# Two layers of sliding-window attention and MLP: W2's transfers, three evictions, masks and sums in other places of a hand-written order

## The chip, the cores and the metric

The kernel runs on one core of one Trainium2 chip. The metric is the time of one execution on the device, in microseconds (us). A core has five engines with a queue of instructions each: TensorE (PE: matrix products and transposes), VectorE (DVE), ScalarE (ACT), GpSimd (POOL) and SyncE (SP), which here only issues DMA transfers. Each engine takes its instructions strictly in order, and waits on semaphores for what the others produce.

## What is computed

The input `x` is 2048 rows of 512 numbers in bf16. Two layers, each of attention and an MLP, are applied one after the other, with the same weights:

```python
def _A_ref(x, wqkv, wo):                      # H = 32 heads of Dh = 16, window W = 256
    q, k, v = ...                             # x @ wqkv, split by head
    scores = jnp.einsum("bhqd,bhkd->bhqk", q, k) * (Dh ** -0.5)
    mask = (idx[:, None] - idx[None, :] >= 0) & (idx[:, None] - idx[None, :] < W)
    scores = jnp.where(mask[None, None], scores, -1e9)
    p = _softmax(scores, axis=-1)
    o = jnp.einsum("bhqk,bhkd->bhqd", p, v)
    return ... @ wo

def _B_ref(x, w1, b1, w2, b2):                # 512 -> 1792 -> 512
    h = _gelu(jnp.einsum("bsd,df->bsf", x, w1) + b1)
    return jnp.einsum("bsf,fd->bsd", h, w2) + b2

x = A_x
x = x + _A_ref(_layernorm(x), A_wqkv, A_wo)
x = x + _B_ref(_layernorm(x), B_w1, B_b1, B_w2, B_b2)
x = x + _A_ref(_layernorm(x), A_wqkv, A_wo)
x = x + _B_ref(_layernorm(x), B_w1, B_b1, B_w2, B_b2)
```

## The kernel before

**Blocks and jobs.** Each attention layer is cut into 8 blocks of 256 rows, so blocks 0 to 7 are layer one and 8 to 15 layer two. A block has two row tiles of 128 rows; row tiles are numbered 0 to 31 over both layers. The MLP goes by jobs of two or four row tiles. The normalizations are numbered 0 to 31 ahead of attention and 32 to 63 ahead of the MLP, so 32, 33 and 48 belong to MLP rows and 8, 9 and 25 to attention rows.

**One block of attention**, with the names that the prediction uses (`b` the block, `tau` the row tile, `k` the normalization):

- `bs`, `ba`, `ve`/`vp`, `pw`: statistics, mean and variance, and the reciprocal root of a row tile. `xn{k}` (L606, DVE) is the normalized tile, `tx{k}` (L611, SP) the DMA that transposes it into `xnTA` (ahead of attention) or `xnTB` (ahead of the MLP).
- `q{b}_{i}`, `k{b}_{i}`, `v{tau}`: the projections (`pe_group`, L632, PE). Each goes into one bank of PSUM and is evicted: `qe{b}_{i}` to `QT` and `ve{tau}` to `Va` by a copy, either VectorE's (L573, in the profile CAST) or ScalarE's (L575, ACTIVATE); `ke{b}_{i}` to `KT` (L666, DVE) with a multiplication by a mask of parities. `vs{tau}_{h}` (L681, SP) are two DMAs that copy `Va` shifted by 64 rows to `Vs`.
- `sc{b}_{g}`: the scores of visit `g` (L733, PE) into four banks, two for each of the two exponentials `ex{b}_{g}_{0,1}` (L740, ACT, 128x1024 to `E`). `mk{b}_{g}_{n}` (L761) multiplies parts of `E` by the mask, on VectorE or GpSimd. A block has 10 visits (5 in the first block of a layer).
- `pv{b}_{cp}`: the product with V for one half of the heads (L783, PE), after half of the visits; then `od` (L792, DVE transpose out of PSUM), `rc` (L796, reciprocal), `nm` (L800, division, DVE or POOL) and `ot` (L806, DVE transpose to `OT`).
- `op{tau}`: the product with Wo (L632), and `rs{tau}` (L832, DVE), which adds it to `X`.

**One job of the MLP.** Each of 14 columns of W1 gives a bank; the gelu is `ge{J}_{fc}` (L863, ACT), or `gb` (L855, DVE, the bias) followed by `ga` (L858, ACT). `y{tau}.{fc}` are the 14 matmuls with W2 (L632); `xb{tau}` (L871, POOL) prepares X plus the bias, and `ya{tau}` (L875, DVE) adds it to the product.

**Loads.** All weights are loaded once. W2 comes in four parts `ldz0` to `ldz3` (L563, SP): rows fc 0–3, 4–7, 8–10 and 11–13. SP's queue also holds every `tx` and `vs`. It issues in order, and a DMA takes one of eight semaphores in turn, so it first waits for the DMA eight places ahead of it.

**What sets the order.** The code registers 3080 nodes, each with an engine, its reads and its writes. `_ORDER` (from L167) is a list, written out, of all 3080 numbers; `_Plan.run` takes the nodes in this order, `_Sched.op` (L62) puts each behind the others of its engine and adds the waits that its data need. So `_ORDER` sets the order in every engine's queue, though a change in it that does not swap two nodes of one engine changes nothing. `_ALT` (from L323) lists the nodes that take their other engine: a copy of an eviction then goes from VectorE to ScalarE, a mask from VectorE to GpSimd, a variance from GpSimd to VectorE. `_BANKS` is the list of PSUM banks in the order in which they are taken.

**The places that are touched**, by queue. In block 1, `sc1_7` follows `sc1_6` in TensorE's queue and takes the banks of `ex1_5` and of `od1_0`. On ScalarE before it stand ex1_4_0, ex1_4_1, ex1_5_1, ex1_5_0, qe3_0, ex1_6_1, ex1_6_0, ex1_7_0. Later in that stage TensorE does k4_0 (needs `xn8`, `tx8`), then job 0's `ge0_9` ends, `y1` (14 matmuls) and `pv1_1` follow. In block 10 VectorE does xn48, rs19 and mk10_4_0, then ke11_1; TensorE has sc10_5, which waits for rs19, and sc10_6, which waits for ke11_1.

Of the kernel before, what the change touches and what calls it, by code (L numbers as in the profile page):

```python
# [19 lines left out]
class _Sched:  # L20
# [300 lines left out]
]  # L321

_ALT = [  # L323
# [623 lines left out]
```

## Time and profile before

| | before |
|---|---|
| time, median of 3 runs | 456.76 us (456.69 to 457.06) |
| time of the profiled execution | 457.15 us |
| its span (first to last instruction in the trace) | 455.3 us |
| mean clock granted to TensorE | 0.996 |
| instructions | 16,821 |
| DMA packets | 47,972, 23.25 MB |
| slices of the 40 in which TensorE is busy under 80% | four: the 10th (5 tenths), 11th, 12th and 16th (7 tenths) |

The profile is one execution of the kernel on the chip. A line of a group of instructions names the engine, the line of the kernel, the operation, the tile written and read, the shape, the count, and behind a bar the time; in the timeline a line begins with its start in us and its duration, and ends, in square brackets, with the idle time of the engine ahead of it and the work that ended it. Where lines are grouped, `x4` is a count, and the duration is that of the whole group.

### The profile page before, as it was taken

How to read it: one execution, taken by the hardware profiler on the slowest of the kernel's cores; microseconds unless marked ns; L12 is line 12 of the kernel's file. 1: busy time of each engine (PE TensorE's matmuls, PEld its weight loads, DVE VectorE, ACT ScalarE, POOL GpSimd, SP SyncE). 2: the span in 40 equal slices, each digit the busy share in tenths (PEclk: the TensorE clock that was granted, in tenths of full speed). 3: DMA queues.
4: the chain of work that ended last, by engine and by line, in shares of the span. 5: the costliest groups of instructions: out<-in, count | busy, mean ns of one | idle time of the engine just before them, and what ended most of it. 6: DMA issues, size and time to landing. Idle time of an engine off the chain costs nothing.

```text
span 455.3 us, 16821 instructions
## 1 busy us (share of the span) xinstructions
PE 420.6 (92%) x7506; PEld 230.2 (51%) x7579; DVE 352.7 (77%) x655; ACT 385.0 (85%) x456; POOL 193.4 (42%) x217
## 2 busy tenths in 40 slices
PE   8998999985779997899999999999999999999997
PEld 4564646543344553445455454555554454444673
DVE  5999689886775778894799867977897598756862
ACT  2997968987889899789998998999888989899633
POOL 4164634237331247632472754274243443526130
PEclk9999999999899999999999999999999999999999
DMA  8695311201400211310012021010232003002110
GB/s 243 186 218 166 77 33 24 44 10 18 86 15 1 25 23 41 76 26 1 14 35 58 1 56 37 10 42 3 62 50 62 1 4 79 14 1 67 60 48 24
DMA packets 47972, 23.25 MB, mean 51 GB/s; under 512 B 33180, under 2 KB 47900, under 8 KB 47900
## 3 DMA queue, kind: packets, MB, share of 16 engines
q1 hardware_dynamic: 47900, 22.17, 21.0%
q8 instruction: 60, 0.98, 0.9%
q14 instruction: 12, 0.10, 0.1%
HBM read 8.00 MB, written 2.10 MB: 22 GB/s over the span
## 4 chain that ended last, share of the span: by engine, by line
PE 69%; DVE 15%; ACT 12%; issue 3%; DMA 2%; POOL 0%; SPq 0%
PE ps L632 52%; ACT E L740 11%; PE ps L733 8%; PE ps L783 7%; DVE KT L666 2%; DVE E L761 2%; DVE OD L792 2%; DVE xn L606 2%; PE ps L525 1%; DVE stat L584 1%; DMA xnTB<-xn 1%; DVE OT L806 1%; DVE X L832 1%; DMA xnTA<-xn 1%; DVE X L875 1%
## 5 line engine op out<-in xcount | busy, mean ns | idle before, releaser
L740 ACT ACTIVATE E<-ps 128x1024 bf16<-128x1024 f32 x300 | 283.1, 1041 | 42.4 <-PE ps L733 41.7
L761 POOL TENSOR_TENSOR E<-E,mask 128x512 bf16<-128x512 bf16 (+2 forms) x97 | 104.2, 1089 | 88.1 <-ACT E L740 88.0
L632 PE MATMUL ps<-xnTB,W_sb 128*128 128x512 bf16 (+1 forms) x542 | 110.2, 335 | 4.2 <-issue 1.6
L632 PE MATMUL ps<-W_sb,gT 128*128 128x512 bf16 x415 | 110.1, 380 | 3.3 <-issue 2.2
L761 DVE TENSOR_TENSOR E<-E,mask 128x512 bf16<-128x512 bf16 (+2 forms) x139 | 70.1, 529 | 10.3 <-ACT E L740 10.1
L632 PE MATMUL ps<-xnTA,Wqkv_sb 128*128 128x256 bf16 x512 | 74.6, 273 | 2.1 <-ACT E L740 0.7
L632 PEld LDWEIGHTS ps<-xnTB,W_sb 128*128 128x128 bf16 x560 | 50.6, 97 | 44.7 <-issue 4.1
L733 PE MATMUL ps<-QT,KT 32*128 32x128 bf16 (+3 forms) x1920 | 60.4, 232 | 10.9 <-ACT E L740 2.9
L632 PEld LDWEIGHTS ps<-W_sb,gT 128*128 128x128 bf16 x448 | 39.6, 98 | 43.2 <-issue 3.6
L733 PEld LDWEIGHTS ps<-QT,KT 32*128 32x128 bf16 x1920 | 28.6, 93 | 62.5 <-ACT E L740 36.9
L632 PEld LDWEIGHTS ps<-xnTA,Wqkv_sb 128*128 128x128 bf16 x512 | 46.9, 98 | 25.3 <-issue 3.9
L792 DVE STREAM_TRANSPOSE OD<-ps 128x1024 f32<-128x1024 f32 x32 | 39.8, 1244 | 21.5 <-PE ps L783 21.2
L863 ACT ACTIVATE gT<-ps,b1T 128x512 bf16<-128x512 f32 (+1 forms) x80 | 43.6, 609 | 10.3 <-PE ps L632 9.9
L871 POOL TENSOR_TENSOR Xb<-X,b2all 128x512 f32<-128x512 bf16 x32 | 38.5, 1209 | 24.8 <-DVE X L875 24.8
L783 PE MATMUL ps<-E,Va 64*17 64x128 bf16 (+3 forms) x1920 | 44.0, 230 | 4.1 <-ACT E L740 1.8
L666 DVE TENSOR_TENSOR KT<-ps,parmask 128x1024 bf16<-128x1024 f32 x32 | 38.8, 1212 | 11.1 <-PE ps L632 10.8
L783 PE MATMUL ps<-E,Vs 64*17 64x128 bf16 (+3 forms) x1920 | 44.6, 230 | 0.0
L783 PEld LDWEIGHTS ps<-E,Va 64*17 64x17 bf16 x1920 | 37.4, 84 | 13.9 <-issue 8.8
L584 DVE BATCH_NORM_STATS2 stat<-X 128x6 f32<-128x512 bf16 x64 | 42.7, 677 | 1.8 <-DMA X<-in_A_x_dram 1.7
L855 DVE TENSOR_SCALAR gT<-ps,b1T 128x512 bf16<-128x512 f32 (+1 forms) x60 | 36.5, 629 | 7.0 <-PE ps L632 6.4
L800 POOL TENSOR_TENSOR Nb<-OD,Rc 128x512 bf16<-128x512 f32 x19 | 20.2, 1061 | 49.9 <-DVE Rc L796 39.6
L632 PE MATMUL ps<-Wo_sb,OT 128*128 128x512 bf16 x120 | 37.2, 388 | 3.4 <-DVE OT L806 2.5
(50 smaller groups left out, 363.0 us busy)
## 6 DMA issues: line engine op xcount, KB each, us to landing
Vs<-Va SPq DMA_DIRECT2D x64, 68.0 KB, 2.1
W_sb<-in_B_w_dram SPq DMA_DIRECT2D x4, 512.0 KB, 5.5
out_dram<-X SPq DMA_DIRECT2D x16, 128.0 KB, 1.9
X<-in_A_x_dram SPq DMA_DIRECT2D x3, 512.0 KB, 7.3
Wqkv_sb<-in_A_wqkv_dram SPq DMA_DIRECT2D x4, 256.0 KB, 5.3
W_sb<-in_B_w_dram SPq DMA_DIRECT2D x1, 768.0 KB, 6.5
W_sb<-in_B_w_dram SPq DMA_DIRECT2D x2, 384.0 KB, 4.8
Wqkv_sb<-in_A_wqkv_dram SPq DMA_DIRECT2D x1, 512.0 KB, 7.1
```

The lines of the kernel that those rows point to most:

```text
L584: add("dve", lambda e, B, t=t, k6=k6: e.bn_stats(stat6[:, k6, :], X[:, t, :]), reads=["X%d" % t], writes=["st%d" % k6], key="bs%d" % (k + j))
L632: r = e.matmul(ps[:, B[g][0], cols], lhsT, rhs, start=st, stop=sp)
L666: add("dve", lambda e, B, g=g, i=i: e.tensor_tensor(out=KT[:, kb, 2 * i : 2 * i + 2].rearrange("p c m a q -> p a (c m) q"), in0=ps[:, B[g] ...
L733: x = e.matmul(ps[:, bk[r], o : o + n], KT[rows, kb, c, m].rearrange("p a q -> p (a q)"), QT[rows, c, q : q + n], start=True, stop=True)
L740: add("act", lambda e, B, g_=g_, gi=gi: e.activation(E[:, 2 * gi : 2 * gi + 2, e0 : e0 + 512], ps[:, B[g_][0] : B[g_][0] + 2, :], AF.Exp, ...
L761: fn = lambda e, B: e.tensor_tensor(out=Ew, in0=Ew, in1=Mw, op=ALU.mult)
L783: x = e.matmul(ps[32 * r : 32 * r + VW, B[g][par], c % 2 * 2 * P + lo : c % 2 * 2 * P + hi], V[rows, (2 * b + m // 2) % VR, c * HC + 2 * r ...
L792: add("dve", lambda e, B: e.transpose(OD[:, s].rearrange("p a c q -> p (a c q)"), ps[:, B[g][0] : B[g][0] + 2, :]), reads=["ps:" + g], wri ...
L800: return e.tensor_tensor(out=Nb[:, s, :].rearrange("p (k a d) -> p a k d", a=2, d=Dh), in0=sums[:, :, :, 0:Dh], in1=rc[:, :, :, None].to_b ...
L855: add("dve", lambda e, B, g=g, fc=fc: e.tensor_scalar(out=gT[:, fc, c0 : c0 + M], in0=ps[:, B[g][0], 0:M], scalar1=b1T[:, fc : fc + 1], sc ...
L863: add("act", lambda e, B, g=g, fc=fc: e.activation(gT[:, fc, c0 : c0 + M], ps[:, B[g][0], 0:M], AF.Gelu_apprx_tanh, bias=b1T[:, fc : fc + ...
L871: add("pool", lambda e, B, t=t, xs=xs: e.tensor_tensor(out=Xb[:, xs, :], in0=X[:, t, :], in1=b2all[:], op=ALU.add), reads=["X%d" % t, "b2a ...
```

## The change

No instruction is added or removed but for those that go to another engine; TensorE's queue and the PSUM banks are the same. By queue:

- **To another engine** (`_ALT`): `ve5` and `qe3_1`, copies of 128x512 out of PSUM, from VectorE to ScalarE; `mk10_3_0`, a mask of block 10, from GpSimd back to VectorE.
- **ScalarE**: `qe3_0` moves ahead of the exponentials ex1_5, `ve5` takes the place behind them, and `qe3_1` stands behind ex1_6. The order is then ex1_4_1, qe3_0, ex1_5_1, ex1_5_0, ve5, ex1_6_1, ex1_6_0, qe3_1, ex1_7_0.
- **VectorE, the first 45 us**: `i6` (a constant) ahead of te3, `ba7` and `ba6` some five places earlier, `ve1` four places later, bs33 ahead of bs32.
- **GpSimd, block 1**: `xb1` and `mk1_7_0` from ahead of mk1_6_0 to behind mk1_5_0. The order is then nm1_0, mk1_6_0, xb0, mk1_8_0, mk1_8_1, mk1_5_0, xb1, mk1_7_0, mk1_7_1.
- **SP, loads of W2**: before, ldz1, ldz2, ldz0, tx32, tx33, vs5_0, vs6_0, vs5_1, tx9, tx8, ldz3, vs4_1, vs7_1; after, tx32, tx33, ldz0, ldz1, vs5_0, vs6_0, vs5_1, tx9, tx8, ldz2, ldz3, vs4_1, vs7_1.
- **VectorE, block 10**: after, xn48, `mk10_3_0`, rs19, bs51, bs50, ba51, vp26, `mk10_4_0`, ba50, vp50, ke11_1; before, mk10_4_0 stood straight behind rs19.
- **VectorE, other blocks**: xn25 ahead of od9_1, `ot11_0` ahead of the masks mk12_2_0 and mk12_0_0 (straight behind od11_1), xn56 ahead of ya21.

The other moves in `_ORDER` swap nodes of different engines only. The diff, cut to the stretches named here (node numbers: ldz0 to ldz3 50 to 53, tx32 242, tx33 244, qe3_0 336, qe3_1 341, ve5 191, xb1 306, mk1_7_0 405, mk10_3_0 2066, mk10_4_0 2071, rs19 1854, ot11_0 2197, xn56 2503, xn25 2014):

```diff
--- before.py
+++ after.py
@@ -165,42 +165,42 @@
...
-    384, 234, 378, 185, 228, 385, 332, 229, 333, 51, 383, 342, 187, 386, 52, 334, 235, 377, 343, 335, 50, 237, 344,
-    337, 394, 388, 345, 396, 382, 338, 188, 238, 236, 387, 189, 239, 190, 395, 346, 339, 240, 389, 336, 191, 398, 243,
-    641, 347, 400, 348, 349, 241, 340, 350, 390, 399, 242, 352, 359, 527, 244, 402, 391, 341, 392, 351, 353, 192, 403,
-    354, 306, 355, 360, 356, 361, 404, 407, 639, 357, 362, 409, 363, 193, 248, 405, 249, 262, 528, 250, 263, 408, 412,
...
+    234, 378, 185, 228, 385, 332, 229, 333, 383, 342, 187, 237, 386, 334, 377, 343, 335, 235, 344, 336, 337, 388, 394,
+    345, 382, 396, 338, 238, 236, 188, 387, 189, 239, 190, 346, 395, 339, 240, 389, 191, 243, 641, 398, 241, 347, 400,
+    390, 348, 242, 349, 340, 350, 399, 352, 527, 359, 244, 391, 351, 341, 392, 402, 353, 403, 354, 50, 355, 401, 360,
+    356, 361, 404, 407, 639, 51, 362, 290, 409, 363, 248, 192, 249, 262, 357, 250, 263, 408, 412, 193, 264, 252, 393,
...
+    279, 275, 564, 640, 416, 276, 428, 306, 272, 52, 415, 422, 287, 53, 281, 282, 284, 186, 405, 288, 285, 365, 277,
...
@@ -248,11 +248,11 @@
-    2070, 1849, 1851, 1744, 2067, 1760, 1852, 2127, 1853, 1741, 2066, 2069, 1619, 1854, 1761, 1742, 1620, 1621, 1762,
-    2071, 1770, 2072, 2078, 1857, 1771, 2079, 1622, 1855, 1623, 1624, 1772, 1858, 2130, 2080, 1763, 1773, 1856, 1859,
+    2070, 1849, 1851, 1744, 2067, 1760, 1852, 2127, 1853, 1741, 2069, 1619, 2066, 1761, 1742, 1854, 1620, 1621, 1762,
+    2072, 1770, 1857, 2078, 1855, 1771, 2079, 1622, 1623, 1858, 1624, 2130, 1772, 2071, 2080, 1763, 1773, 1856, 1859,
...
@@ -321,14 +321,14 @@
 _ALT = [
-    60, 66, 74, 79, 108, 112, 120, 125, 164, 169, 184, 210, 219, 336, 369, 373, 377, 378, 383, 392, 397, 401, 405, 406,
+    60, 66, 74, 79, 108, 112, 120, 125, 164, 169, 184, 191, 210, 219, 336, 341, 369, 373, 377, 378, 383, 392, 397, 401,
...
-    1859, 2040, 2053, 2062, 2066, 2067, 2072, 2076, 2081, 2095, 2104, 2130, 2160, 2167, 2173, 2177, 2187, 2191, 2192,
+    1838, 1843, 1859, 2040, 2053, 2062, 2067, 2072, 2076, 2081, 2095, 2104, 2130, 2160, 2167, 2173, 2177, 2187, 2191,
```

109 rows, old and new, of tables (_ALT, _ORDER) are left out of this document.

## The prediction

> **What bounds the kernel now.** I read the page first, then the waits, the chain of waits, and the timeline of the places where the edits fall. The page:
>
> ```profile
> span 455.3 us, 16821 instructions
> PE 420.6 (92%) x7506; PEld 230.2 (51%) x7579; DVE 352.7 (77%) x655; ACT 385.0 (85%) x456; POOL 193.4 (42%) x217
> PE 69%; DVE 15%; ACT 12%; issue 3%; DMA 2%; POOL 0%; SPq 0%
> ```
>
> TensorE carries the end: 69% of the chain of waits. Every edit is on another queue, and the order of TensorE is the same before and after, so an edit counts only where TensorE waits for VectorE, ScalarE or a transfer. The stretches of the edits (columns: busy time and instructions of each engine, clock, DMA share, GB/s):
>
> ```profile
> core 0: us, PE busy (x) PEld busy (x) DVE busy (x) ACT busy (x) POOL busy (x), PEclk, DMA share, GB/s
> 39.10:44.30 5.20, 3.29 (x37) 1.40 (x36) 4.97 (x9) 3.48 (x5) 2.23 (x3) 1.00 0.34 74
> 53.50:58.00 4.50, 4.41 (x148) 3.13 (x148) 1.82 (x2) 3.38 (x6) 0.00 (x0) 1.00 0.01 2
> 267.80:277.20 9.40, 8.52 (x211) 5.02 (x214) 9.29 (x18) 6.86 (x8) 5.98 (x7) 1.00 0.22 45
> ```
>
> From 39.1 to 44.3 VectorE works 4.97 of 5.20 us and TensorE only 3.29: here VectorE leads. From 267.8 to 277.2 it works 9.29 of 9.40. From 53.5 TensorE is full again. The two VectorE stretches decide this case.
>
> **Block 1, three evictions to ScalarE.** ve5 and qe3_1 leave VectorE for ScalarE, and qe3_0 (already there) moves one place ahead.
>
> ```profile
> 35.28 1.94 ACT L740 ACTIVATE E<-ps 128x1024 bf16<-128x1024 f32 x2 [0.66 <-PE ps L733]
> 37.11 0.60 ACT L575 ACTIVATE QT<-ps 128x512 bf16<-128x512 f32 x1
> 38.56 1.94 ACT L740 ACTIVATE E<-ps 128x1024 bf16<-128x1024 f32 x2 [0.85 <-PE ps L733]
> 42.22 1.02 ACT L740 ACTIVATE E<-ps 128x1024 bf16<-128x1024 f32 x1 [1.72 <-PE ps L733]
> ...
> 37.43 0.68 DVE L573 CAST Va<-ps 128x512 bf16<-128x512 f32 x1
> 39.26 1.24 DVE L792 STREAM_TRANSPOSE OD<-ps 128x1024 f32<-128x1024 f32 x1
> 40.98 0.63 DVE L573 CAST QT<-ps 128x512 bf16<-128x512 f32 x1
> ...
> 41.77 0.40 PE L733 MATMUL ps<-QT,KT 32*128 32x192 bf16 x12 [1.53 <-DVE QT L573]
> ```
>
> VectorE loses 0.68 + 0.63 us. ScalarE takes 0.60 for each in idle time of 0.66, 0.85 and 1.72 us: qe3_0 goes into the first, ve5 takes qe3_0's old place at 37.11, and qe3_1 goes into the third, from 40.4 to 41.0. The scores at 41.77 are sc1_7. By the code they need banks 0 to 3, which the exponentials from 38.56 and od1_0 at 39.26 give back, both at 40.50. The 1.53 us ended with qe3_1 (40.98 + 0.63 = 41.61), though qe3_1 frees bank 5, which sc1_7 does not write. So either the profile's reading holds and VectorE's queue released it, or something that no view names held TensorE, such as its instruction stream, which comes over the same 16 DMA engines as W2:
>
> ```profile
> q8 instruction: 60, 0.98, 0.9%
> ...
> W_sb<-in_B_w_dram SPq DMA_DIRECT2D x4, 512.0 KB, 5.5
> W_sb<-in_B_w_dram SPq DMA_DIRECT2D x2, 384.0 KB, 4.8
> ...
> 33.07 2.47 SPq L563 DMA_DIRECT2D W_sb<-in_B_w_dram  x3
> 39.42 2.51 SPq L611 DMA_TRANSPOSE xnTB<-xn  x2
> 41.98 2.86 SPq L681 DMA_DIRECT2D Vs<-Va  x3
> ...
> 50.18 0.59 SPq L563 DMA_DIRECT2D W_sb<-in_B_w_dram  x1
> ```
>
> Three parts of W2 (1.4 MB), issued from 33.07 to 35.54, take about 5 us each to land, so they run until about 40, just ahead of that wait. After the change none of them runs then. By either reading the wait goes. What is late next is the pair of exponentials that ends at 40.50: sc1_7 at about 40.6, and with its 0.40 us and the semaphore the exponential from 42.22 starts near 41.08. **Gain there 1.14 us**; qe3_1 is done at 41.0, so ScalarE does not hold it.
>
> **Block 1, what keeps the 1.14 and adds to it.** At the end of the stage TensorE waits once more, for a transposed row:
>
> ```profile
> 47.54 1.33 DVE L606 TENSOR_SCALAR xn<-X,statmv,rstd 128x512 bf16<-128x512 bf16 x1
> ...
> 270.11 0.41 DVE L606 TENSOR_SCALAR xn<-X,statmv,rstd 128x512 bf16<-128x512 bf16 x1
> ...
> 47.58 1.15 POOL L761 TENSOR_TENSOR E<-E,mask 128x512 bf16<-128x512 bf16 x1
> ...
> 48.95 3.09 DMA xnTA<-xn
> ...
> 51.30 0.38 PE L632 MATMUL ps<-Wo_sb,OT 128*128 128x512 bf16 x1
> 52.08 0.39 PE L632 MATMUL ps<-xnTA,Wqkv_sb 128*128 128x256 bf16 x2 [0.40 <-DMA xnTA<-xn]
> ...
> 50.99 0.47 ACT L863 ACTIVATE gT<-ps,b1T 128x256 bf16<-128x256 f32 x1
> 53.30 1.17 ACT L858 ACTIVATE gT<-gT 128x512 bf16<-128x512 bf16 x2
> ...
> 54.92 1.67 PE L632 MATMUL ps<-W_sb,gT 128*128 128x512 bf16 x7
> ```
>
> xn8 takes 1.33 us where the same form takes 0.41 (the row at 270.11, of block 10): it starts at 47.54, GpSimd's mask at 47.58, and it ends at 48.87, 0.14 after that mask (48.73). GpSimd holds something that xn8 needs. xb1 and mk1_7_0 now come after mk1_5_0, so other masks stand beside xn8, which starts near 46.40. It waits between nothing much and one mask of 1.15 us: end between 46.85 and 47.95. I take 46.85, since the masks ahead of it now start earlier. Its transpose lands about 3.1 us later, at 50.1 (at worst 51.1); TensorE gets there near 50.0; and ge0_9, which frees the bank, ends at 51.46 - 1.14 = 50.32. So k4_0 starts near 50.4 instead of 52.08. ScalarE, busy without a gap from 42.22 on but for the table load, then limits: y1.2, at the head of the row of 54.92, needs the gelu that ends at 54.47, 0.45 earlier, of which some 0.05 goes for the semaphore. So the gain there is at most 1.14 + 0.40 = 1.5. I take **1.4 us** for block 1, with 1.0 (xn8 behind a whole mask) and 1.5 as bounds.
>
> The Trainium skill's "SBUF — State Buffer", section "Who interferes with whom", says that VectorE and GpSimd share one pair of SBUF ports, and that the first to start blocks the other fully. The rows of xn8 and its mask agree. The page adds that a VectorE tensor_tensor with two SBUF inputs meets the same lock, which speaks against moving the mask of block 10 to VectorE; the third rival prices this.
>
> **W2 behind the transposes.** tx32 and tx33 start when xn32 and xn33 are ready (39.42; about 38.8 after), so nothing is gained by being ahead of the loads. ldz0 and ldz1 issue near 41.3 and land by about 47 (5.5 us); their first users are y1's matmuls, in the row of 54.92 and one shortly ahead of it, some 5 us later even when they come 1.5 us earlier. ldz2 follows tx8, near 48.2, and lands by 53.5 (4.8 us with the issues); its first user, y1.8, stands behind pv1_1, so after 54.92 + 1.67 = 56.6, or 55.2 after the change. Cost 0: the cover is k4, q4 and pv1_1, and with less than 1.7 us of it left y1 would wait for the rest. Two loads of 0.59 us each now stand in SP's queue ahead of vs5_0, vs6_0 and tx9; the queue stood idle for vs6_0 inside the row at 41.98 (2.86 for three, 0.59 each), so tx9 still issues near 44.4. The two parts behind tx8 delay only vs4_1 and vs7_1, which block 2 reads near 70.
>
> **Block 10, a mask to VectorE.** mk10_3_0 leaves GpSimd, and mk10_4_0 goes four places back, behind the sums.
>
> ```profile
> 269.78 0.42 DVE L761 TENSOR_TENSOR E<-E,mask 128x512 bf16<-128x512 bf16 x1
> ...
> 271.18 1.23 DVE L606 TENSOR_SCALAR xn<-X,statmv,rstd 128x512 bf16<-128x512 bf16 x1
> 272.33 0.67 DVE L832 TENSOR_TENSOR X<-X,ps 128x512 bf16<-128x512 bf16 x1
> 272.92 1.43 DVE L761 TENSOR_TENSOR E<-E,mask 128x768 bf16<-128x768 bf16 x1
> 275.89 1.22 DVE L666 TENSOR_TENSOR KT<-ps,parmask 128x1024 bf16<-128x1024 f32 x1
> ...
> 271.11 1.15 POOL L761 TENSOR_TENSOR E<-E,mask 128x512 bf16<-128x512 bf16 x1
> 272.31 1.63 POOL L761 TENSOR_TENSOR E<-E,mask 128x768 bf16<-128x768 bf16 x1
> ...
> 273.15 0.40 PE L733 MATMUL ps<-QT,KT 32*128 32x256 bf16 x8 [0.32 <-DVE X L832]
> 277.16 0.40 PE L733 MATMUL ps<-QT,KT 32*128 32x256 bf16 x8 [0.40 <-DVE KT L666]
> ```
>
> xn48 pays 0.82 us (1.23 for 0.41) behind mk10_3_0 on GpSimd, and mk10_4_0 pays 0.8 behind mk10_4_1 (1.43 against at most 0.63, which is 0.42 for 768 in place of 512). With mk10_3_0 on VectorE: xn48 ends at 271.6, mk10_3_0 at 271.93 (0.42), rs19 at 272.5 instead of 273.00, and sc10_5 loses its 0.32. mk10_4_0 now starts near 273.9, just as mk10_4_1 ends (273.94), at its bare 0.6. VectorE saves 0.82 + 0.8 - 0.42 = 1.2 us up to ke11_1. TensorE cannot use all of that: it sat 0.32 us for rs19 and 0.40 us for ke11_1, and with both gone sc10_6 comes 0.72 earlier. **Gain 0.7 us**, bounds 0 (see the third rival) and 1.2.
>
> **The rest at nothing**: xn25 ahead of od9_1, xn56 ahead of ya21, ot11_0 ahead of two masks all stand before VectorE instructions that wait for TensorE, so that wait covers them; without it 0.3 to 0.7 each. The normalization sums ba6, ba7, bs32 and bs33, and i6 and ve1 only change places among VectorE's first 45 us; I bound them together at -0.2 to +0.2, one sum of some 0.1 to 0.2 either way.
>
> **Sum.** The profiled execution took 457.15 us (its span of 455.3 and 1.85 around it). 457.15 - 1.4 - 0.7 = 455.05. The median of the runs shown is 456.76, 0.39 lower, so **454.7 us**.
>
> **The rivals.**
> First, the wait at 41.77 stays, as its cause is neither named. Then ScalarE's dense stretch does not move, and only xn8 helps: 0.40 at y1.2, with 0.7 from block 10: 456.76 - 1.1 = 455.7. For it: sc1_7's own inputs were ready at 40.50. Against: both candidates are removed.
> Second, slower. The four parts of W2 run in 41 to 47 and 49 to 53.5, and the instruction fetches wait behind them: 60 packets in 455 us, one in 7.6. If TensorE then runs dry twice, for 1.5 us as at 41.77, the loss is 3.0 against 2.1: 457.7. It decides from 2.1 us in all. For it: the odd wait just behind the first W2 loads. Against: loads behind the transposes meet a stage of 37 matmul records in 5.2 us, which drains instructions slowly; the danger is pv1_1 in the dense row from 53.50. The Trainium skill's "Runtime: NRT & Kernel Launch", section "Instruction fetch mechanics", calls this fetch mostly hidden; no row here shows it directly.
> Third, block 10 gives nothing or takes: if xn48 ends 0.7 us later than I think, mk10_3_0 meets mk10_4_1 (from 272.31) and rs19 starts behind it at 274.0, 1.7 us later than now, of which sc10_5 and all that follows loses some 1.3: 456.76 - 1.4 + 1.3 = 456.7. With no gain it is 455.4. Against: 0.4 us lie between mk10_3_0's end and that start.
> Fourth, the gains are eaten later in TensorE's full stages, as on paper nothing else moved: 456.7. Against: with the loads over, every wait after 58 is set by another engine's work, which moves along.
>
> **How the numbers follow.** Forecast 0.55 (454.1 to 455.3), first rival 0.13, second 0.12, third 0.14, fourth 0.06. The range leaves out the second alone (0.12), since the third and the fourth end at 456.7: 453.9 (456.76 - 1.5 - 1.2 = 454.06, less 0.2 for the small moves) to 456.7. A measurement of this kernel tells 0.2%, 0.9 us, from no change. Faster by that (below 455.85): the forecast, most of the first (0.11) and the milder half of the third (0.07), 0.73. Slower: the second, 0.12. Within: 0.15.
>
> **What would show it.** The exponential behind sc1_7 starts near 41.1 after a ScalarE wait of well under 1 us; xn8 takes under 0.6 us; k4_0 starts near 50.4 and no W2 matmul of y1 waits for a DMA; pv1_1 comes 1.4 us earlier. In block 10 xn48 takes 0.4, sc10_5 waits for nothing, and sc10_6 comes 2.1 us earlier than 277.16. I am wrong if the wait of sc1_7 keeps its length, if TensorE shows a new idle time with no releaser between 50 and 58, or if mk10_3_0 takes over 1 us on VectorE.

## The result and the profile after

| | before | after |
|---|---|---|
| median of 10 runs each, side by side | 456.97 us | 455.83 us (454.67 to 456.69) |
| ratio, 95% interval | | 0.9968 (0.9958 to 0.9978) |
| profiled execution, its span | 457.15, 455.3 us | 456.14, 454.3 us |
| two later comparisons of the same kernel, in the experiments | | 0.9946 (0.9930 to 0.9963), 0.9972 (0.9960 to 0.9985) |

The kernel became faster by some 0.3%: 1.1 us in the first comparison, where 2.1 were forecast. Its executions differ among themselves: all 28 of the three comparisons lie between 453.5 and 457.0 us, median 455.6. That scatter turns out to be part of the answer.

The page of the changed kernel, the lines that stand against those of before:

```profile
span 454.3 us, 16895 instructions
PE 432.0 (95%) x7579; PEld 230.6 (51%) x7579; DVE 350.6 (77%) x654; ACT 386.5 (85%) x458; POOL 191.9 (42%) x216
q8 instruction: 60, 0.98, 1.0%
PE 76%; ACT 10%; DVE 9%; DMA 3%; issue 1%; SPq 0%; POOL 0%
```

In the chain of waits VectorE's share falls from 15% to 9%, TensorE's rises from 69% to 76%, and transfers rise from 2% to 3%. The same stretch of block 1 as before, in the view by windows:

```profile
core 0: us, PE busy (x) PEld busy (x) DVE busy (x) ACT busy (x) POOL busy (x), PEclk, DMA share, GB/s
39.10:44.30 5.20, 3.54 (x39) 1.43 (x37) 4.38 (x7) 5.18 (x7) 3.27 (x3) 1.00 0.75 97
```

VectorE has 0.6 us less to do there and ScalarE now works without a break, but TensorE does hardly more in the stretch than before (37 weight loads against 36), and the transfers' share went from 0.34 to 0.75. The timeline shows why:

```profile
40.14 1.26 SPq L611 DMA_TRANSPOSE xnTB<-xn  x1
40.47 0.60 ACT L575 ACTIVATE QT<-ps 128x512 bf16<-128x512 f32 x1
40.64 0.40 PE L733 MATMUL ps<-QT,KT 32*128 32x192 bf16 x12 [0.31 <-ACT E L740]
41.09 3.77 ACT L740 ACTIVATE E<-ps 128x1024 bf16<-128x1024 f32 x4
41.45 1.67 SPq L563 DMA_DIRECT2D W_sb<-in_B_w_dram  x2
44.32 1.03 PE L632 MATMUL ps<-xnTB,W_sb 128*128 128x256 bf16 x8 [1.34 <-DMA xnTB<-xn]
47.56 0.42 DVE L606 TENSOR_SCALAR xn<-X,statmv,rstd 128x512 bf16<-128x512 bf16 x1
51.63 1.58 PE L632 MATMUL ps<-xnTA,Wqkv_sb 128*128 128x256 bf16 x13
```

sc1_7 starts at 40.64 instead of 41.77 and its exponential at 41.09, which is the forecast (41.08) within 0.01. Then TensorE meets m0_1.0, the first product of the MLP. It needs tx33, the transpose issued at 40.14, and waits 1.34 us for it. Its first weight load starts at 44.29, against 44.27 before: the whole 1.1 us is given back at one matmul. In the view of transfers, the window of that one issue:

```profile
xnTB<-xn SPq DMA_TRANSPOSE x1, 4.1
```

and in the kernel before, from 40.6 to 40.8, where tx32 still counts in:

```profile
xnTB<-xn SPq DMA_TRANSPOSE x2, 2.5
```

That is 4.1 us from issue to landing, where the same transpose took 2.5 before. Further on k4_0 starts 0.47 us earlier than before (51.60 for 52.07) and pv1_1 too (56.06 for 56.53); that is what block 1 brought in this execution. Block 10:

```profile
270.27 0.38 DVE L606 TENSOR_SCALAR xn<-X,statmv,rstd 128x512 bf16<-128x512 bf16 x1
270.57 0.42 DVE L761 TENSOR_TENSOR E<-E,mask 128x512 bf16<-128x512 bf16 x1
270.90 0.68 DVE L832 TENSOR_TENSOR X<-X,ps 128x512 bf16<-128x512 bf16 x1
271.85 0.40 PE L733 MATMUL ps<-QT,KT 32*128 32x256 bf16 x8
272.95 0.55 DVE L761 TENSOR_TENSOR E<-E,mask 128x768 bf16<-128x768 bf16 x1
275.39 0.40 PE L733 MATMUL ps<-QT,KT 32*128 32x256 bf16 x8
```

All of it as forecast: xn48 takes 0.38 instead of 1.23, the mask that came from GpSimd 0.42, mk10_4_0 0.55 instead of 1.43, and neither sc10_5 nor sc10_6 waits for VectorE. From sc10_4 to sc10_6 it is 0.86 us less than before. One loss comes later, at k14_0, again a wait for a transpose:

```profile
331.69 0.38 PE L632 MATMUL ps<-xnTA,Wqkv_sb 128*128 128x256 bf16 x2 [0.33 <-DMA xnTA<-xn]
```

Before, tx29 had landed in time there; from y16.1 to k14_0 the changed kernel takes 0.65 us more, though no edit touches that place.

### The profile page after: what moved, and what is told of

Same layout as the page of the kernel before. It is cut to its first block, busy times and chain, and to the rows that moved or that the text cites. A ratio compares the mean times of both kernels' runs of the same rounds, so it can differ in the third digit from the quotient of the medians.

```text
span 454.3 us, 16895 instructions
## 1 busy us (share of the span) xinstructions
PE 432.0 (95%) x7579; PEld 230.6 (51%) x7579; DVE 350.6 (77%) x654; ACT 386.5 (85%) x458; POOL 191.9 (42%) x216
## 4 chain that ended last, share of the span: by engine, by line
PE 76%; ACT 10%; DVE 9%; DMA 3%; issue 1%; SPq 0%; POOL 0%
PE ps L632 58%; ACT E L740 9%; PE ps L733 8%; PE ps L783 8%; DVE E L761 2%; DVE OD L792 2%; DMA xnTB<-xn 2%; PE ps L525 1%; DVE KT L666 1%; DMA xnTA<-xn 1%; DVE stat L584 1%; DVE xn L606 1%; DVE OT L806 1%; DVE Nb L800 0%; DVE X L832 0%
## 5 line engine op out<-in xcount | busy, mean ns | idle before, releaser
L761 POOL TENSOR_TENSOR E<-E,mask 128x512 bf16<-128x512 bf16 (+2 forms) x96 | 102.9, 1085 | 93.9 <-ACT E L740 93.7
L632 PE MATMUL ps<-W_sb,gT 128*128 128x512 bf16 x448 | 118.1, 380 | 0.3 <-issue 0.3
L632 PE MATMUL ps<-xnTB,W_sb 128*128 128x512 bf16 (+1 forms) x560 | 114.6, 337 | 2.6 <-DMA xnTB<-xn 1.5
L761 DVE TENSOR_TENSOR E<-E,mask 128x512 bf16<-128x512 bf16 (+2 forms) x140 | 69.0, 517 | 10.9 <-ACT E L740 10.7
L632 PEld LDWEIGHTS ps<-W_sb,gT 128*128 128x128 bf16 x448 | 39.5, 97 | 43.7 <-issue 4.0
L792 DVE STREAM_TRANSPOSE OD<-ps 128x1024 f32<-128x1024 f32 x32 | 39.8, 1244 | 20.2 <-PE ps L783 19.8
L783 PEld LDWEIGHTS ps<-E,Va 64*17 64x17 bf16 x1920 | 37.2, 84 | 12.7 <-issue 10.1
L632 PE MATMUL ps<-Wo_sb,OT 128*128 128x512 bf16 x128 | 39.9, 390 | 1.7 <-DVE OT L806 1.6
L800 POOL TENSOR_TENSOR Nb<-OD,Rc 128x512 bf16<-128x512 f32 x19 | 20.1, 1058 | 48.7 <-DVE Rc L796 40.5
```

The source lines that it names most:

```text
L632: r = e.matmul(ps[:, B[g][0], cols], lhsT, rhs, start=st, stop=sp)
L761: fn = lambda e, B: e.tensor_tensor(out=Ew, in0=Ew, in1=Mw, op=ALU.mult)
L783: x = e.matmul(ps[32 * r : 32 * r + VW, B[g][par], c % 2 * 2 * P + lo : c % 2 * 2 * P + hi], V[rows, (2 * b + m // 2) % VR, c * HC + 2 * r ...
L792: add("dve", lambda e, B: e.transpose(OD[:, s].rearrange("p a c q -> p (a c q)"), ps[:, B[g][0] : B[g][0] + 2, :]), reads=["ps:" + g], wri ...
L800: return e.tensor_tensor(out=Nb[:, s, :].rearrange("p (k a d) -> p a k d", a=2, d=Dh), in0=sums[:, :, :, 0:Dh], in1=rc[:, :, :, None].to_b ...
```

## The experiments

The theories. **A**: the wait ahead of sc1_7 was TensorE's own instruction stream: the packets of queue q8 (60 of them, 0.98 MB, so 16 KB each; TensorE has 7579 weight loads, as many matmuls and some 160 waits, so one packet for about 255 instructions) came late behind W2's loads. **B**: VectorE's queue with qe3_1 was the wait, as the profile names it. **C**: the 1.1 us were given back since W2's parts, now right behind tx33, slow its landing.

**W2's places alone.** The edit, in names, in the list of the kernel before:

```diff
 SP: vs4_0
-ldz1 ldz2 ldz0
 tx32 tx33
+ldz0 ldz1
 vs5_0 vs6_0 vs5_1 tx9 tx8
+ldz2
 ldz3
```

> The kernel before with W2's parts alone behind the transposes; VectorE and ScalarE keep their queues of before. Theory A (W2's loads held the fetch of TensorE's instructions, and that was the wait of 1.5 us ahead of sc1_7): the wait goes, sc1_7 starts near 40.6 instead of 41.74. Theory B (the profile's reading: VectorE's queue with qe3_1 held it): sc1_7 stays at 41.6 to 41.8. By both, tx33 lands late with two parts of W2 right behind it (4.1 us after its issue in the changed kernel, 2.5 before), xn33 is as late as before, and m0_1.0 starts between 44.3 and 45.0. So A's gain is given back before 45, and the time is 457.0 to 457.6 by A and by B (no gain, perhaps 0.5 us worse).

**The evictions alone.**

```diff
 ACT: ex1_4_1
+qe3_0
 ex1_5_1 ex1_5_0
-qe3_0
+ve5
 ex1_6_1 ex1_6_0
+qe3_1
 ex1_7_0
```

> The kernel before with the three evictions on ScalarE alone; W2's parts stay ahead of the transposes. Theory A (instruction fetch behind W2's loads): the fetch still comes near 39.0, and sc1_7 still starts between 41.5 and 41.8, with both exponentials and od1_0 done by 40.6. Theory B (VectorE's queue): sc1_7 starts near 40.6 to 41.1. m0_1.0, with tx33 landing in 2.5 us and half a us earlier, starts near 44.2 by A, and near 43.0 by B, which would be worth 1 us of the whole.

With W2 alone: 455.82 us, ratio 0.9962 (0.9951 to 0.9974). With the evictions alone: 456.40 us, 0.9986 (0.9969 to 1.0003). The timeline with W2 alone, qe3_1 still on VectorE:

```profile
39.97 0.40 PE L733 MATMUL ps<-QT,KT 32*128 32x192 bf16 x12 [0.46 <-DVE OD L792]
40.29 0.63 DVE L573 CAST QT<-ps 128x512 bf16<-128x512 f32 x1
42.66 1.04 PE L632 MATMUL ps<-xnTB,W_sb 128*128 128x256 bf16 x8
```

sc1_7 starts 0.3 us *before* qe3_1 does. So qe3_1 cannot have been its wait, and B falls. With the evictions alone qe3_1 runs on ScalarE at 40.33, and yet:

```profile
40.33 0.61 ACT L575 ACTIVATE QT<-ps 128x512 bf16<-128x512 f32 x1
42.53 0.62 PE L733 MATMUL ps<-QT,KT 32*128 32x192 bf16 x12 [2.35 <-issue]
```

2.35 us of "issue", which is time in which the engine waited for nothing that the profile shows. (This profile's execution took 459.2 us, against a median of 456.40; but the wait stands in the same place in the kernel before and with block 10 alone.) The view of transfers, in windows of 1 us, has the packet that comes ahead of this place (packets, MB, share of the engines). With the evictions alone it lies in 39.5 to 40.5:

```profile
q8 instruction: 1, 0.02, 7.1%
```

and with W2 alone in 36.5 to 37.5:

```profile
q8 instruction: 1, 0.02, 7.0%
```

In the 14 traces of this case that packet starts late (38.96 to 39.92 us) in the three where three parts of W2 are issued from 33 on, and early (36.93 to 38.05) in the eleven others. From TensorE's entry into the 256 instructions ahead (most of them a product with V, entered at 36.0 to 37.2) to the packet it is 2.0 to 3.1 us in those three and 0.8 to 1.4 us in the eleven. In 13 of the traces sc1_7 starts 2.58 to 2.91 us after the packet; in the last experiment, where the packets end 16 instructions earlier, it is a matmul ahead of sc1_7 that does. In eight of the 13 sc1_7 also starts within 0.15 us of the last exponential or of od1_0, which free its banks, so there its distance from the packet proves nothing. In the other five, the three late ones among them, both were done 0.4 to 2.1 us earlier and the packet came 2.58 to 2.78 us before sc1_7. A fits, and the last experiment tests it by itself.

What I missed in the expectation: with W2 alone tx33 was not late (2.5 us, m0_1.0 at 42.53), and the gain was kept up to there. So C, as I had it, falls too: the same two loads stood right behind tx33. But 0.6 us of it went at the next input: xn8 took 0.92 us, k4_0 waited for tx8 and came 8.36 us behind m0_1.0 (7.80 before, 7.31 in the changed kernel), so pv1_1 was only 0.45 us closer to sc1_6 than before.

**W2's first parts two places later; the changed kernel once more; the evictions back.** Three edits of the changed kernel: ldz0 and ldz1 behind vs6_0; none; and ve5 and qe3_1 back on VectorE.

```diff
 SP: tx32 tx33
-ldz0 ldz1
 vs5_0 vs6_0
+ldz0 ldz1
 vs5_1 tx9 tx8 ldz2 ldz3
```

> The changed kernel with ldz0 and ldz1 two places later, behind vs6_0 in place of right behind tx33. Theory C (the gain at sc1_7 was given back at m0_1.0 since the two parts of W2 slowed tx33's landing from 2.5 to 4.1 us): tx33 lands near 42.7, m0_1.0 starts near 42.9 to 43.2 instead of 44.29, ScalarE's gaps of 0.90 and 1.31 ahead of ex1_9 and ge0_9 shrink, pv1_1 comes some 0.7 to 1.0 us earlier (55.1 to 55.4) and the time is 0.5 to 1.0 us under the changed kernel's: 454.9 to 455.4. Rival D (the loads slow whatever stands beside them, so the loss only moves to tx9 and tx8, or to the first users of W2): pv1_1 stays at 55.9 or later and the time within 0.3 us of the changed kernel's 455.8.

> The changed kernel once more, for a second profile. Two of its losses may be of one execution only: tx33 took 4.10 us to land in its profile (2.47 with the same SP queue in the kernel with W2's places alone), and k14_0 waited 0.89 us for a transpose that took 4.06 us. If they are, this profile shows tx33 at 2.4 to 2.6 us and m0_1.0 about 2.5 us behind sc1_7, as in the others. If the loads right behind tx33 cause it each time, tx33 takes 4 us again and m0_1.0 comes 3.6 us behind sc1_7. The time 455.4 to 456.2.

> The changed kernel with ve5 and qe3_1 back on VectorE. If the instruction fetch was the wait ahead of sc1_7 and W2's new places removed it, the two copies off VectorE are worth little at sc1_7 (0.1 us: od1_0 then ends 0.15 us after ex1_6_0 instead of 0.5 before) and up to 0.5 us at xn8 and tx8: time 0 to 0.5 us over the changed kernel's, 455.8 to 456.3. If VectorE's queue was the wait, sc1_7 waits for qe3_1 again and starts over 3 us behind sc1_6: time 456.6 or more.

ldz0 and ldz1 later: 455.66 us, 0.9965 (0.9952 to 0.9979); tx33 in 2.50 us, m0_1.0 2.5 us behind sc1_7, but tx8 now runs beside both loads and takes 3.95 us, and k4_0 starts 1.28 us behind the matmul ahead of it. From sc1_6 to pv1_1 its trace has 17.57 us, 0.3 less than the first profile of the changed kernel, and the median, beside the changed kernel's 455.03 to 455.83 in other comparisons, shows nothing of that. The changed kernel again: 455.03 us, and tx33 again late (4.13 us, m0_1.0 3.8 us behind sc1_7). Evictions back on VectorE: 455.77 us, 0.9968 (0.9954 to 0.9982), 0.7 us above the changed kernel of the same comparison, though the two intervals overlap; tx33 in 2.48 us, but xn8 takes 1.31 us and k4_0 comes 8.19 us behind m0_1.0, for 7.31 with the evictions on ScalarE. So neither edit by itself explains the late tx33: with W2 alone it is on time, with the evictions alone it is late with no part of W2 behind it (the last one ahead of it landed at 41.98). What it does go with is the next packet of instructions:

```
                                   tx33 issued   packet     tx33 takes   m0_1.0 behind sc1_7
changed, first profile                40.14       41.66        4.10          3.65
changed, second profile               39.66       40.84        4.13          3.78
changed, eight matmuls more           40.52       41.79        3.94          2.72
changed, GpSimd order of before       40.14       41.51        3.73          3.37
changed, third profile                39.87       46.14        2.49          2.54
W2 alone                              40.00       42.62        2.47          2.59
ldz0, ldz1 two places later           39.28       43.42        2.50          2.53
evictions back                        40.23       44.79        2.48          2.53
before                                40.67       45.31        2.51          2.53
block 10 alone                        40.68       45.50        2.52          2.53
W2 split (below)                      39.40       43.42        2.48          2.53
evictions alone                       39.81       39.92        3.61          3.25
evictions alone, tx32                 38.56       39.92        4.04
```

(Times in us from the start of each trace.) Where the packet starts 0.1 to 1.5 us after the transpose's issue, the transpose takes 3.6 to 4.1 us; where the packet comes after the transpose has landed, 2.5. (In the two traces of the version with one part early tx33's landing is not recorded; the packet comes 3.0 and 4.1 us after its issue, and m0_1.0 stands 2.5 us behind sc1_7.) Over all transposes after 60 us in the 14 traces, with tx33, those with a packet 0.3 to 2.6 us after their issue take over 3.5 us in 49% of 173 cases, those without in 5% of 405. That is a coincidence counted in traces, not an edit that moves a packet alone; why the one or the other comes first stays open.

**The changed kernel a third time, and a version with one part of W2 early.** The edit of the latter, against the changed kernel:

```diff
 SP: vs4_0
+ldz0
 tx32 tx33
-ldz0 ldz1
 vs5_0 vs6_0
+ldz1
 vs5_1 tx9 tx8 ldz2 ldz3
```

> The changed kernel with ldz0 early (behind vs4_0, near 32.6), ldz1 behind vs6_0, and ldz2 and ldz3 behind tx8 as in the changed kernel. Theory: one part alone early lands by 37.5 and does not hold the packet that q8 brings near 37.9, so sc1_7 starts 2.5 us behind sc1_6 as in the changed kernel; with one part beside tx9 and tx8 in place of two, tx8 lands in 2.8 us as where ldz0 alone stood there, and with two parts behind tx8 in place of three, the packet that pv1_1 needs is not held (it was for 2.9 us there). tx33 takes 2.5 us. pv1_1 then comes 16.8 us behind sc1_6 (17.87 in the changed kernel's first profile) and takes 1.2 us; time 1.0 us under the changed kernel's: 454.0 to 454.8. Rival: the early part holds the packet near 37.9, sc1_7 starts over 3 us behind sc1_6 and the time is 455.5 or more.

> The changed kernel a third time, beside the version with one part of W2 early (ldz0 behind vs4_0, ldz1 behind vs6_0) on the same chip. tx33 lands in 3.7 to 4.2 us again, since a packet of TensorE's instructions comes 1.2 to 1.5 us after its issue, as in all four profiles with two parts of W2 right behind tx33 and the evictions on ScalarE; m0_1.0 comes 3.4 to 3.8 us behind sc1_7. Time 454.8 to 455.8.

> The version with one part of W2 early once more, for a direct comparison. tx33 in 2.5 us, m0_1.0 2.5 us behind sc1_7, pv1_1 16.8 us behind sc1_6 and so 1.1 us earlier than in the changed kernel. If nothing later takes this back, its median is 0.7 to 1.2 us under the changed kernel's of this call; if TensorE's later stages take it back, the two medians lie within 0.4 us.

The third profile of the changed kernel missed my expectation, and shows more than a repetition would have. In the timeline:

```profile
40.72 0.40 PE L733 MATMUL ps<-QT,KT 32*128 32x192 bf16 x12 [0.75 <-ACT QT L575]
43.26 1.03 PE L632 MATMUL ps<-xnTB,W_sb 128*128 128x256 bf16 x8 [0.19 <-ACT E L740]
```

and in the view of transfers, in the windows from 39.8 to 40.0 and from 324.8 to 325.0:

```profile
xnTB<-xn SPq DMA_TRANSPOSE x2, 2.5
...
xnTA<-xn SPq DMA_TRANSPOSE x1, 2.4
```

tx33 lands on time, m0_1.0 waits 0.19 us for a bank and not for a transfer, tx29 lands on time too, and this execution took 453.51 us: the same kernel as that of 456.14, 2.6 us apart. The version with one part early was run twice: 454.77 us, 0.9955 (0.9938 to 0.9973), and, beside the changed kernel's 455.53 (0.9972), 454.20 us, 0.9949 (0.9932 to 0.9966). In both its profiles m0_1.0 comes 2.5 us behind sc1_7, as where tx33 is on time, sc1_7 starts 2.4 us behind sc1_6 and pv1_1 16.72 and 16.78 us behind it (17.87 in the first profile after, 18.43 before), all as expected. It is 1.3 us under the changed kernel by the medians of one comparison; the two intervals just overlap.

**W2 split, and GpSimd's order back.** From the changed kernel, ldz0 alone behind vs6_0 and the three others behind tx8; and xb1 and mk1_7_0 back in their places of before.

```diff
 SP: tx33
-ldz0 ldz1
 vs5_0 vs6_0
+ldz0
 vs5_1 tx9 tx8
+ldz1
 ldz2 ldz3
```

> The changed kernel with ldz0 alone in the stage (behind vs6_0) and ldz1, ldz2 and ldz3 behind tx8. In the kernel with ldz0 and ldz1 behind vs6_0, tx8 took 3.95 us to land and k4_0 waited 1.28 us for it. Theory (W2's loads slow the transposes that run beside them): tx8 lands in 2.4 to 3.0 us, k4_0 waits under 0.7 us for it and pv1_1 comes 0.4 to 0.7 us earlier behind sc1_6 than there (17.57 us there): 16.9 to 17.2; time 455.0 to 455.4. Rival: the late part ldz1 reaches y1.4 too late, TensorE waits there, and pv1_1 does not gain: time 455.6 or more.

```diff
 POOL: nm1_0
+xb1 mk1_7_0
 mk1_6_0 xb0 mk1_8_0 mk1_8_1 mk1_5_0
-xb1 mk1_7_0
 mk1_7_1
```

> The changed kernel with xb1 and mk1_7_0 back in their places of before on GpSimd, ahead of mk1_6_0. If the move of the two is what freed xn8 (0.42 us in the changed kernel, 1.33 before), xn8 takes 0.9 to 1.4 us again behind mk1_8_0, tx8 issues 0.5 to 0.9 us later, and k4_0 with it: time 0.3 to 0.6 us over the changed kernel's. Rival: xn8 was freed by coming earlier, and the GpSimd order matters little: xn8 under 0.6 us and the time within 0.2 us of the changed kernel's.

The split is slower than the kernel before: 457.69 us, 1.0020 (1.0006 to 1.0034), and its trace shows two losses that neither the theory nor its rival had. tx8 does land in 2.8 us, and pv1_1 starts 16.75 us behind sc1_6. But then pv1_1, which takes 1.2 us elsewhere, stops in the middle:

```profile
55.10 0.22 PE L783 MATMUL ps<-E,Vs 64*17 64x128 bf16 x1
56.43 0.23 PE L783 MATMUL ps<-E,Vs 64*17 64x128 bf16 x3 [1.10 <-issue]
```

Both rows are matmuls of one node; no semaphore stands between them. In the windows from 50.5 to 53 the view of transfers has no packet on q8, and from 53 to 54.5 one:

```profile
q8 instruction: 1, 0.02, 5.4%
```

It starts at 53.67, 2.76 us ahead of 56.43 and 3.0 us after TensorE entered the 256 instructions ahead; in the three profiles of the changed kernel the same packet comes 0.7 to 0.9 us after that. Three parts of W2 were issued from 47.4 to 49.0 and land at 51.6 to 54.3. This is my second rival, in the place that it named. The Trainium skill's "Runtime: NRT & Kernel Launch", section "Instruction fetch mechanics", has blocks of 256 instructions and calls the cost of crossing from one to the next mostly hidden. The count above agrees with the blocks; here the crossing is not hidden, 1.1 us in the middle of one node.

The second loss is as large, at a wait for a transpose of the MLP:

```profile
126.66 1.04 PE L632 MATMUL ps<-xnTB,W_sb 128*128 128x512 bf16 x4 [1.71 <-DMA xnTB<-xn]
```

That transpose took 4.06 us, with a packet 1.89 us after its issue; in the changed kernel's first two profiles the packet came 2.3 and 3.0 us after it, and it took 2.4. Against the second profile of the changed kernel the split loses 1.3 us at pv1_1 and 1.4 us here. The profiled execution took 456.53 us; what makes the median 1.2 us longer no trace shows.

GpSimd's old order costs nothing: 454.67 us (0.9938, 0.9915 to 0.9962) against 455.03 for the changed kernel of the same comparison, the intervals overlapping. xn8 still takes 0.46 us, as it starts at 47.21 with only 0.3 us of mk1_8_0 left.

**Block 10 alone**, in the kernel before.

```diff
 DVE: xn48
+mk10_3_0
 rs19
-mk10_4_0
 bs51 bs50 ba51 vp26
+mk10_4_0
 ba50 vp50 ke11_1
 POOL: mk10_3_1
-mk10_3_0
 mk10_4_1
```

> The kernel before with mk10_3_0 on VectorE and mk10_4_0 behind the sums, nothing else. My step: xn48 at 0.4 us, sc10_6 some 0.8 us earlier than in the kernel before (277.16 on its own clock), and the time 0.7 us lower, 456.2 to 456.4. Rival: the gain is taken back at a later transfer (the changed kernel gave back 0.65 at k14_0), and the time stays within 0.3 us of before.

455.93 us, 0.9967 (0.9955 to 0.9979). In its trace sc10_4 to sc10_6 is 0.86 us shorter, the same 0.86 as in every profile with this edit. The median fell by more, 1.5 us; its profile ends only 0.95 us earlier than that of before, so the rest is the scatter between executions or something that I did not find. The three parts do not add up either: by their ratios W2 alone, the evictions alone and block 10 alone take off 0.38, 0.14 and 0.33%, 0.85% together, and the changed kernel, which has them all, 0.28 to 0.54% in its three comparisons. The late tx33 and k14_0 account for a part of that at most; the runs do not show the rest.

**Eight small matmuls more.** The changed kernel with 16 instructions added to the warm-up near 5 us, so that every later packet ends 16 instructions earlier in the program.

```diff
-add("pe", lambda e, B, bk=h % 8: e.matmul(ps[:, bk, :], gT[:, 0, 0:P], gT[:, 0, :], start=True, stop=True),
+def warm(e, bk, h):
+    if h == 9:
+        for _ in range(8):
+            e.matmul(ps[0:16, bk, 0:16], gT[:, 0, 0:16], gT[:, 0, 0:16], start=True, stop=True)
+    return e.matmul(ps[:, bk, :], gT[:, 0, 0:P], gT[:, 0, :], start=True, stop=True)
+add("pe", lambda e, B, bk=h % 8, h=h: warm(e, bk, h),
```

> The changed kernel with eight matmuls of 16 columns (16 instructions with their weight loads) added to the warm-up at 5 us; all else the same. Queue q8 brings TensorE's instructions in packets of 16 KB, one per 256 of them, and in all the profiles so far TensorE never takes the first instruction of a packet less than 3.4 us after it took the first one of the packet before. Theory A (TensorE waits for these packets): every packet now ends 16 instructions earlier in the program, and where a product with V of 256 instructions, done in 1.2 us, follows a packet's start, the next one comes too late. From the times of the instructions in the changed kernel's profile, with 3.6 us asked for from packet to packet, I work out new waits of 1.5 us near 39, 1.6 near 111, 1.6 near 189, 0.7 near 266, 1.4 near 308, 1.9 near 396 and 1.4 near 429: 10 us in all, time 463 to 468. Rival B (the packets are fetched well ahead and TensorE waits for the engines alone): the eight matmuls cost what they take, under 0.8 us, and the time is 455 to 456.8.

459.24 us, 1.0059 (1.0037 to 1.0080): 3.4 to 4.2 us above the changed kernel's three medians. Of the seven places that I had worked out, five have a new wait; three of them (this kernel's lines are 6 higher):

```profile
40.60 0.83 PE L638 MATMUL ps<-xnTA,Wqkv_sb 128*128 128x256 bf16 x6 [1.17 <-issue]
...
113.52 0.40 PE L739 MATMUL ps<-QT,KT 32*128 32x256 bf16 x8 [1.75 <-DVE xn L612]
...
400.79 0.38 PE L638 MATMUL ps<-xnTB,W_sb 128*128 128x512 bf16 x1 [1.97 <-issue]
```

Each stands 256 instructions behind the first one of a packet, with a product with V in between. Two are put down to "issue", one to a VectorE instruction. Counted from TensorE's first (weight loads, matmuls and waits), the instructions at the five new waits, at 40.59, 113.51, 311.88, 400.56 and 434.27, have the numbers 1217, 3777, 10,690, 14,017 and 15,042: multiples of 256 apart, within one. In the other kernels sc1_7 has 1218, and the matmul at 56.43 in the split 1730, which is 512 more. The size was half of the expected 10 us: after such a wait part of it is won back at the next wait for another engine (of the 1.4 us at 40.59 nothing is left at m0_1.0, where the changed kernel had its own wait for tx33). Nor is all of it waits for packets: at 128.47 TensorE waits 1.9 us for a transpose, which the changed kernel's profiles do not. Theory A is confirmed without any change to loads or evictions: eight matmuls that take under 1 us cost some 4.

## Why the prediction was right, and where it was wrong

**Direction and range** held: 455.83 lies between 453.9 and 456.7. The forecast itself, 454.7, was 1.1 us low for the first comparison, 0.9 for the median of all 28 executions.

**The wait at sc1_7** went by 1.1 us, as forecast, and by the second of the two readings that I left open, the instruction stream. The three evictions did not remove it: alone they left it in full. So "here VectorE leads" was wrong for this wait. The evictions are worth 0.7 us in the medians of one comparison, with overlapping intervals, and by the traces 0.9 us at k4_0, by way of xn8 and tx8.

**The step that failed** is "W2 behind the transposes ... Cost 0", together with "What is late next is the pair of exponentials". I covered W2's own users and SP's queue, and asked of tx32 and tx33 only when they start. Who waits for tx33 I didn't ask: m0_1.0, which before started 1.1 us after tx33 had landed (43.18), a margin as large as the gain. After the change there was none left, and tx33 itself took 1.6 us longer in two of three profiles. There block 1 brought 0.56 and 0.44 us (pv1_1 behind sc1_6: 17.87 and 17.99 for 18.43); in the third, with tx33 on time, 1.27 us, inside the bounds of 1.0 and 1.5. So the mechanism of block 1 was right, and the term was too large for the executions in which a packet meets tx33. A slip in the working changed nothing: TensorE "gets there near 50.0" is by its own rows 51.68 - 1.14 = 50.54.

**xn8** is 0.42 us as forecast (0.45), but not because other masks stand beside it: with GpSimd's old order it is 0.46 too. It is a matter of when it starts.

**Block 10** was right step by step, its size 0.86 for the forecast 0.7. The third rival, a mask that meets another on GpSimd, did not happen: 0.37 us lay between, for the 0.4 that I had.

**The rest at nothing** can't be told more closely than the scatter: from pv1_1 to sc10_4 the three profiles of the changed kernel take 212.3 to 212.9 us, the four without the small moves (before, W2 alone, the evictions alone, block 10 alone) 212.9 to 213.5. None of the small moves was tried alone.

**The second rival** did not come true in the changed kernel, but it is real: one more load behind tx8 sets it off. I had 3.0 us for two such waits; one was 1.1 us.

**k14_0** was in no step. It costs 0.6 to 0.8 us in the nine profiles in which a packet comes 1.8 to 2.1 us after tx29's issue (W2 alone and the evictions alone are among them), and nothing in the five others, those of the kernel before, of block 10 alone and the third one after among them. So it is no effect of an edit near it, but goes with where the packet falls; no part of W2 is under way there.

**The total** lies in the range in part by luck. In the first pair of profiles block 1 gave 0.56 us and block 10 0.86, 1.4 of the forecast 2.1; the stretch between them gave 0.45 where I had nothing, and from sc10_6 to k14_0 the changed kernel lost 0.93. Neither of these two was forecast, and they partly cancel.

## What to carry to other kernels

A gain ahead of a wait is worth only the margin to the next input of the same queue: list for the first few instructions behind it when each of their inputs landed, transfers among them, before adding the gain to the sum. When an engine idles and the profile names a releaser that the instruction doesn't depend on, or "issue", look at the instruction queue among the transfers, and at what large transfers were issued just ahead of its packet. In a kernel whose TensorE runs some thousands of small matmuls in microseconds, bulk loads belong into stretches where neither a transpose nor a needed packet is under way, and adding or removing a few instructions early shifts all later packets, so small edits should be compared over many executions.

## What the runs showed of the hardware that I had not expected

At the places where nothing else held it (sc1_7 in five traces, pv1_1 in the split, the five new waits with eight matmuls more), TensorE took the first instruction behind a packet 2.2 to 2.8 us after the packet started. Ahead of sc1_7 the packet started 0.8 to 1.4 us after TensorE had entered the 256 instructions before it, and 2.0 to 3.1 us after where three parts of W2 had been issued. By the sum of the smaller figures, 256 instructions that run in less than some 3 to 4 us leave TensorE waiting, and eight matmuls in the warm-up decided where. Where a transposing transfer and a packet of instructions came together, one of them was late: tx33 took 3.6 to 4.1 us in place of 2.5, or the packet behind sc1_7 came 2.6 to 5.4 us after TensorE had entered the one ahead, in place of 0.8 to 1.2. Which holds up which, no run here separates.
